# A gated mix of a long convolution and a dilated local attention: the projection's row permutations go to GpSimd's queue, and its last tiles share one buffer

## The chip, the cores and the metric

The kernel runs on one core of a Trainium2 chip. The metric is the device time of one execution in microseconds (us), lower is better. The engines that matter here are TensorE (PE, matrix products), VectorE (DVE) and ScalarE (ACT), which both copy results out of PSUM and do the elementwise work, and two engines that issue transfers here: SyncE (SP) and GpSimd (POOL). Each engine works through its own list of instructions in order, so an instruction that waits holds up everything behind it in its list.

## The reference

The output mixes two branches of the same input, position by position.

```python
x = A_q                                   # [1, 2048, 640]
g = sigmoid((x * gate_w).sum(-1, keepdims=True))
a = q * (irfft(rfft(kv) * rfft(ssm_k)) + kv * ssm_D)   # kv = shifted_conv(k) * v, length 2048 padded to 4096
b = attention(x @ wqkv; 32 heads, window of 8 keys, dilation 2) @ wo
out = g * a + (1 - g) * b
```

Each row of the output thus needs the long convolution's result `y`, times `q` and the gate `g`, plus `(1 - g)` times the row of the projection `b`.

## The kernel before, in words

**The long convolution** is a Fourier transform written as matrix products. The channels go in five groups (`NG = 5`, here g0 to g4). For the data there are per group four units of a first step (`s1_unit`, line 729, source `kv`), four of a second (`s2_unit`, line 747, result in `X[:, 7]`), an elementwise complex product on VectorE (`mults`, lines 866 and 869, four pairs per group), and four units of an inverse step (`inverse1`, line 883). When all of that is done, `inverse2` (line 960) runs over the 16 row positions t, three at a time; its results are copied by ScalarE (line 969), multiplied into `qg` by VectorE (line 972), the projection is added (`adds`, line 1027), and the rows are stored (`store`, line 985). One `X[:, 7]` serves all groups: the second step's copies of g4 may only be written once the products of g3 have been read.

**q** is loaded a second time late (`load_q`, line 923, 16 transfers on SP) into the tile `qg`, which takes the place of `kv`: the load waits for the last unit of the first step, the last reader of `kv`. `qscale` (line 937) multiplies `qg` by the gate on VectorE, 16 instructions.

**The projection** (`outproj`, line 999) makes 16 tiles t, ten matrix products each. ScalarE or VectorE copies a tile, times `1 - g`, into a staging buffer (lines 1010 and 1012). The rows of a tile do not stand on the partitions on which `qg` has them, so each pair of tiles is permuted by four transfers from the staging buffer into the tile `bl` (line 1019), which `adds` then reads. The staging buffer has three places of a pair each: `X[:, 1]` for the first three pairs, then `room`.

**What sets the order.** Nothing is fixed by hand: a planner in plain Python (`Plan`) holds the parts as streams of requests. Every request names an engine ("P", "A", "D", "G" for GpSimd and "S" for SP), a cost in ns, and what it waits for; the planner keeps its own clock per engine and emits next the request with the lowest `start + 120 * priority` (a lower number goes first). Transfers occupy a modelled pipe, and at most eight may be under way for each issuing engine. So a change of an engine, a cost or a priority changes the order of instructions on all engines. PSUM has four places of two banks, which all products share.

Of the kernel before, what the change touches and what calls it, by code (L numbers as in the profile page):

```python
# [10 lines left out]
BF = mybir.dt.bfloat16  # L11
# [6 lines left out]
S = 2048  # L18
# [225 lines left out]
def kernel(  # L244
# [14 lines left out]
    nc = tc.nc  # L259
# [6 lines left out]
    def raw(ap, off, dims):  # L266
        return bass.AP(tensor=ap.tensor, offset=ap.offset + off, ap=dims)
# [11 lines left out]
    def psum(g, name, shape=(128, 2, 512), dt=F32, k=0):  # L279
        t_ = psp.tile(list(shape), dt, name=name, tag=f"ps{g.banks[k]}")  # L280
        return t_
# [11 lines left out]
    G = Gs[:, 0:8192].rearrange("p (a r b) -> p a r b", a=32, r=2)  # L293
# [42 lines left out]
    def ev(name):  # L336
        if name not in E:
            E[name] = Ev()
        return E[name]

    def mark(name, g):
        x = ev(name)
        x.t, x.eng = g.done.t, g.done.eng

    def us(nbytes, run):
        return 1.1 * nbytes / 16.0 / run * (10.0 + run / 24.0)
# [79 lines left out]
    st = {}  # L426
# [145 lines left out]
    def gcol(t):  # L572
        return 8 * (t % 2) + t // 2
# [405 lines left out]
    def store(t):  # L979
        if t in (1, 5):  # L980
            return
        t0 = t - 3 if t < 8 else t - 1
        for gg in range(4):
            eng = nc.gpsimd if t < 8 and gg % 2 else nc.scalar if t == 15 and gg % 2 else nc.sync
            eng.dma_start(raw(outf, (16 * gg + t0) * D, [[64 * D, 32], [1, (t - t0 + 1) * D]]),  # L985
                          st["qg"][32 * gg:32 * gg + 32, t0:t + 1, :].rearrange("p t c -> p (t c)"))

    def outproj():
        yield Req("G", 1.0, [ev("oT"), ev("wo"), ev("gate")])
        oT, wo, bl = st["oT"], st["wo"], st["bl"]  # L990
        stage = None
        for t in range(16):
            u = t // 2
            g = yield Req("P", 1400.0, [ev("i12")] if u >= 6 else [ev("i11")] if u >= 3 else [], take=1, ins=10, pri=8 if t < 6 else None)
            op = psum(g, "op")
            for ft in range(NDT):
                a = oT[:, ft, 0:1]
                for k in range(2):
                    nc.tensor.matmul(op[:, k, 0:320], lhsT=raw(a, HS * (t % 2) + t // 2, [a.ap[0], [8, 128]]),  # L999
                                     rhs=wo[:, ft, 320 * k:320 * k + 320], start=(ft == 0), stop=(ft == NDT - 1))  # L1000
            if u in (3, 6) and t % 2 == 0:
                room = st["p2"].tile([128, 4096], BF, name="room", tag=f"Hs{u // 3}")
                stage = room[:, 0:3840]
            elif t == 0:
                stage = st["X"][:, 1, 0:3840]
            part = stage[:, 1280 * (u % 3):1280 * (u % 3) + 1280].rearrange("p (t c) -> p t c", t=2)
            r = yield Req("AD", dict(A=725.0, D=880.0), [g.done], give=g.banks)
            blt = part[:, t % 2, :].rearrange("p (k c) -> p k c", k=2)
            if r.eng == "A":
                nc.scalar.activation(blt, op[:, :, 0:320], ACT.Copy, scale=omg[:, gcol(t):gcol(t) + 1])  # L1010
            else:
                nc.vector.tensor_scalar(blt, op[:, :, 0:320], omg[:, gcol(t):gcol(t) + 1], None, ALU.mult)
            if t % 2:
                done = r.done
                for gg in range(4):
                    r = yield Req("S", 450.0, [done], move=us(81920, 2560) * 1.5)
                    row = part[gg:gg + 1, 0, 0:1]
                    pitch = row.ap[0][0]
                    nc.sync.dma_start(bl[32 * gg:32 * gg + 32, t - 1:t + 1, :].rearrange("p t c -> p (t c)"),
                                      raw(row, 0, [[4 * pitch, 32], [1, 1280]]))  # L1020
                mark(f"bl{t}", r)

    def adds():
        for t in range(1, 16, 2):
            yield Req("D", 740.0, [ev(f"bl{t}"), ev(f"pr{t}")])
            qg, bl = st["qg"], st["bl"]
            nc.vector.tensor_tensor(qg[:, t - 1:t + 1, :], qg[:, t - 1:t + 1, :], bl[:, t - 1:t + 1, :], ALU.add)  # L1027
            store(t)
# [29 lines left out]
    plan.add(inverse1(), 4)  # L1058
    plan.add(otrans(), 3)
    plan.add(outproj(), 6)  # L1060
    plan.add(load_t(), 0)
    plan.add(load_q(), 1)
# [34 lines left out]
```

## Time and profile before

| what | us |
|---|---|
| median of 3 executions (lowest, highest) | 265.04 (264.39, 267.68) |
| the profiled execution, its own time | 265.23 |
| its span on the core | 263.4 |

The span is what the profile shows from the first to the last instruction; the rest of the profiled execution's time lies around it. The profile's busy times over the span are 214.6 us of PE, 176.2 of DVE, 184.3 of ACT and 51.1 of POOL. These are averages over stages with different limits: the rows of single stretches tell more than the sums.

### The profile page before, as it was taken

The page shows a single profiled execution, that of the slowest core. Times are in us where ns is not written, and L with a number is a line of the kernel's source. Part 1 is how long each engine was busy: PE and PEld are TensorE (multiplying, and loading weights), DVE is VectorE, ACT ScalarE, POOL GpSimd, SP SyncE. Part 2 cuts the span into 40 slices and gives each one's busy share as a digit, 9 for nine tenths or more (in the row PEclk, how much of TensorE's full clock was granted, in tenths as well). Part 3 has the DMA queues.
Part 4 walks back from the last instruction along what each step waited for, and adds up shares of the span by engine and source line. Part 5 has one row for each costly group of instructions (what it writes and reads, how often), then busy time and mean ns, then how long its engine had stood idle before and what let it go on. Part 6 is the DMA issues. An engine that isn't in the chain of part 4 may idle for free.

```text
span 263.4 us, 9665 instructions
## 1 busy us (share of the span) xinstructions
PE 214.6 (81%) x4294; PEld 162.5 (62%) x4294; DVE 176.2 (67%) x223; ACT 184.3 (70%) x220; POOL 51.1 (19%) x107
## 2 busy tenths in 40 slices
PE   7999989999989998888894989999998304996710
PEld 3765544545546675667683888889997204995410
DVE  1658599999998445786785787959851219705851
ACT  4447587577877999999984757889987006886740
POOL 7703704761700643500000000000000000000300
PEclk9999999999999999555579799999999955999575
DMA  6995799877940848989758577415103990111564
GB/s 195 346 357 193 197 281 348 222 183 159 194 130 7 229 92 203 225 146 304 265 124 192 116 146 171 114 55 163 52 2 77 206 170 0 54 50 55 134 194 126
DMA packets 52265, 42.67 MB, mean 162 GB/s; under 512 B 27280, under 2 KB 46864, under 8 KB 52224
## 3 DMA queue, kind: packets, MB, share of 16 engines
q1 hardware_dynamic: 48368, 35.16, 51.5%
q0 software_dynamic: 3760, 6.74, 10.0%
q8 instruction: 33, 0.54, 0.9%
q10 hardware_dynamic: 96, 0.16, 0.2%
q14 instruction: 8, 0.07, 0.1%
HBM read 23.51 MB, written 5.25 MB: 109 GB/s over the span
## 4 chain that ended last, share of the span: by engine, by line
PE 34%; DMA 20%; DVE 18%; issue 14%; ACT 8%; SPq 3%; POOL 2%; DVEq 0%; ACTq 0%; POOLq 0%
PE i L883 8%; DMA qb<-Gs 6%; PE op L999 6%; DMA qg<-in_A_q_dram 5%; PE s L747 5%; ACT ET L670 4%; PE pj L596 3%; PE s L729 3%; DVE pb L474 3%; DVE pa L489 3%; PE psv L534 2%; PE O L696 2%; DVE Hb L273 2%; DVE X L869 2%; DMA Wv<-in_B_wqkv_dram 2%
## 5 line engine op out<-in xcount | busy, mean ns | idle before, releaser
L670 ACT ACTIVATE ET<-sc 128x726 bf16<-128x726 f32 (+1 forms) x80 | 64.5, 865 | 5.5 <-PE sc L662 5.1
L596 PE MATMUL pj<-xT,Wqk 128*128 128x363 bf16 (+3 forms) x250 | 48.4, 343 | 1.8 <-DVE oS L710 1.2
L747 PE MATMUL s<-Am,Gs 64*128 64x64 bf16 x1280 | 30.5, 203 | 21.0 <-ACT X L271 14.1
L747 PEld LDWEIGHTS <-Gs 64*128 64x128 bf16 x1280 | 27.5, 104 | 24.4 <-issue 23.1
L596 PEld LDWEIGHTS <-Wqk 128*128 128x128 bf16 x250 | 23.1, 97 | 20.5 <-DVE oS L710 1.9
L273 DVE CAST Am<-s 128x1024 bf16<-128x1024 f32 x22 | 26.3, 1219 | 7.5 <-PE s L729 7.5
L271 ACT CAST X<-s 128x1024 bf16<-128x1024 f32 x16 | 15.9, 1026 | 16.5 <-DVE X L869 16.5
L985 POOL DMA_DIRECT2D out_dram<-qg x4 | 2.0, 506 | 125.5 <-DVE qg L1027 125.4
L999 PE MATMUL op<-wo,Hb 128*128 128x320 bf16 x160 | 26.4, 314 | 0.0
L534 PE MATMUL psv<-Wv,xT 128*128 128x320 bf16 x170 | 25.2, 299 | 1.0 <-ACT ET L670 0.5
L883 PE MATMUL i<-M,X 128*128 128x128 bf16 x160 | 21.8, 229 | 0.6 <-DVE X L869 0.6
L999 PEld LDWEIGHTS <-Hb 128*128 128x128 bf16 x160 | 21.0, 147 | 1.5
L271 ACT CAST X<-i 128x1024 bf16<-128x1024 f32 x20 | 20.0, 1017 | 2.7 <-PE i L883 2.1
L883 PEld LDWEIGHTS <-X 128*128 128x128 bf16 x160 | 20.6, 150 | 1.3 <-DVE X L869 0.9
L662 PE MATMUL sc<-qb,kb 31*128 31x121 bf16 x544 | 18.6, 245 | 2.7 <-DVE oS L710 1.0
L534 PEld LDWEIGHTS <-xT 128*128 128x128 bf16 x170 | 16.0, 98 | 7.5 <-issue 0.9
L271 ACT CAST Am<-s 128x1024 bf16<-128x1024 f32 x18 | 17.9, 1030 | 2.4 <-PE s L729 2.2
L696 PEld LDWEIGHTS <-ET 128*128 128x128 bf16 x544 | 16.1, 100 | 5.1 <-issue 2.7
L883 PE MATMUL i<-M,Hs 128*128 128x128 bf16 x128 | 18.2, 233 | 0.6 <-ACT Am L271 0.3
L696 PE MATMUL O<-VW,ET 128*128 128x21 bf16 x544 | 16.6, 176 | 2.5 <-ACT ET L670 1.5
L489 DVE TENSOR_TENSOR pa<-pa,pb 128x2560 bf16<-128x2560 bf16 x12 | 17.9, 1489 | 0.3
L662 PEld LDWEIGHTS <-kb 31*128 31x128 bf16 x544 | 10.3, 103 | 12.5 <-issue 8.1
(81 smaller groups left out, 361.0 us busy)
## 6 DMA issues: line engine op xcount, KB each, us to landing
X<-Hs SPq DMA_DIRECT2D x16, 256.0 KB, 4.8
Hb<-in_A_k_dram SPq DMA_DIRECT2D x4, 640.0 KB, 10.4
kv<-in_A_v_dram SPq DMA_DIRECT2D x4, 640.0 KB, 13.5
kv_scr<-Hb SPq DMA_DIRECT2D x8, 320.0 KB, 5.6
Hb<-in_A_ssm_k_dram SPq DMA_DIRECT2D x16, 160.0 KB, 4.2
kv<-kv_scr SPq DMA_DIRECT2D x8, 320.0 KB, 6.6
qg<-in_A_q_dram SPq DMA_DIRECT2D x16, 160.0 KB, 6.0
Gs<-cf_G SPq DMA_DIRECT2D x8, 256.0 KB, 6.8
```

The lines of the kernel that those rows point to most:

```text
L271: nc.scalar.copy(dst, src)
L273: nc.vector.tensor_copy(dst, src)
L474: nc.vector.tensor_tensor(dst[:, t0:t1, :], src, wl[:, j, :].unsqueeze(1).to_broadcast([128, t1 - t0, D]), ALU.mult)
L489: nc.vector.tensor_tensor(pa[:], pa[:], pb[:], ALU.add)
L534: nc.tensor.matmul(ps[:, bb, 0:320], lhsT=xT[:, dt, BP * (b0 + bb):BP * (b0 + bb) + 128], rhs=Wv[:, dt, c0:c0 + 320], start=(dt == 0), sto ...
L596: nc.tensor.matmul(ps[:, i, 0:n], lhsT=Wqk[:, dt, w, 128 * ft:128 * ft + 128], rhs=rhs, start=(dt == 0), stop=(dt == NDT - 1))
L662: nc.tensor.matmul(scs[h4 // 2][:, h4 % 2, BP * bb:BP * bb + BP], lhsT=kb[r:r + DH + NF, 128 * b:128 * b + 128], rhs=qb[r:r + DH + NF, BP ...
L670: nc.scalar.activation(ETs[e][:, :, 0:nw], scs[hf][:, :, 0:nw], ACT.Exp, scale=SCALE)
L696: nc.tensor.matmul(O[:, o0:o0 + 21], lhsT=ET[:, hh, BP * bb:BP * bb + 128], rhs=VW[:, b, 4 * t + h4, :], start=True, stop=True, skip_group ...
L747: nc.tensor.matmul(o, lhsT=G[rows, j, rr, :], rhs=Am[rows, 2 * j + rr, :, :], start=(rr == 0), stop=(rr == 1), tile_position=(64 * c, 0), ...
L883: nc.tensor.matmul(o, lhsT=src[:, c, :, :, 8 * oc + il].rearrange("p q j -> p (q j)"), rhs=M[:, k, :], start=(k == 0), stop=(k == 1), skip ...
L999: nc.tensor.matmul(op[:, k, 0:320], lhsT=raw(a, HS * (t % 2) + t // 2, [a.ap[0], [8, 128]]), rhs=wo[:, ft, 320 * k:320 * k + 320], start=( ...
```

## The change

Three edits. The permuting transfers are issued by GpSimd in place of SP, and are planned on GpSimd's clock and its eight transfers. Four stores (rows up to t = 7) go from GpSimd to SP. The last two pairs of tiles no longer take a third staging buffer but the first two places of `room`, which the pairs of t = 6, 7 and t = 8, 9 used; so their request waits for those pairs' permutations (`bl7`, `bl9`) and not for the inverse step of g2 (`i12`). The request's priority is 8 for t = 6 and 7 (6 before, the stream's own), and 0 for t from 8 on (6 before).

```diff
         for gg in range(4):
-            eng = nc.gpsimd if t < 8 and gg % 2 else nc.scalar if t == 15 and gg % 2 else nc.sync
+            eng = nc.gpsimd if t < 4 and gg % 2 else nc.scalar if t == 15 and gg % 2 else nc.sync
...
-            g = yield Req("P", 1400.0, [ev("i12")] if u >= 6 else [ev("i11")] if u >= 3 else [], take=1, ins=10, pri=8 if t < 6 else None)
+            g = yield Req("P", 1400.0, [ev(f"bl{2 * u - 5}")] if u >= 6 else [ev("i11")] if u >= 3 else [], take=1, ins=10, pri=8 if t < 8 else 0)
...
-            if u in (3, 6) and t % 2 == 0:
-                room = st["p2"].tile([128, 4096], BF, name="room", tag=f"Hs{u // 3}")
+            if t == 6:
+                room = st["p2"].tile([128, 4096], BF, name="room", tag="Hs1")
...
-                    r = yield Req("S", 450.0, [done], move=us(81920, 2560) * 1.5)
+                    r = yield Req("G", 500.0, [done], move=us(81920, 2560) * 1.5)
...
-                    nc.sync.dma_start(bl[32 * gg:32 * gg + 32, t - 1:t + 1, :].rearrange("p t c -> p (t c)"),
+                    nc.gpsimd.dma_start(bl[32 * gg:32 * gg + 32, t - 1:t + 1, :].rearrange("p t c -> p (t c)"),
```

The planner then writes out another order. VectorE's list before, at the place where `kv` has had its last reader (the cast to `Am` is the copy of the last unit of the first step; `Hs` is the product of g3):

```order
L273 CAST X<-s_4233 128x8x128
L273 CAST Am<-s_4303 128x4x64x4
L937 TENSOR_SCALAR qg<-qg,g_nat 128x640 x12
L866 TENSOR_TENSOR Hs<-X,Hs 128x8x128
L869 TENSOR_TENSOR X<-X 128x8x128
```

and of the changed kernel, from the last pair of products of g4 (`sH`) on, which has those of g3 ahead of it:

```order
L866 TENSOR_TENSOR sH<-X,sH 128x8x128
L869 TENSOR_TENSOR X<-X 128x8x128
L937 TENSOR_SCALAR qg<-qg,g_nat 128x640 x16
L972 TENSOR_TENSOR qg<-X,qg 128x3x320 x2
L1027 TENSOR_TENSOR qg<-qg,bl 128x1280
```

All 16 scalings of `qg` now stand behind all the products; before, twelve of them stood ahead of the products of g3, and four ahead of those of g4.

ScalarE's list before, around the copy of the last unit of the first step (`Am<-s_4359`); L1010 is the copy of a projection tile:

```order
L271 CAST X<-s_4314 128x8x128
L1010 ACTIVATE room<-op,omg 128x640
L271 CAST Am<-s_4359 128x4x64x4
L271 CAST X<-s_4395 128x8x128
L271 CAST X<-s_4437 128x8x128
L1010 ACTIVATE room<-op,omg 128x640
L271 CAST X<-s_4486 128x8x128
```

and of the changed kernel, around the same copy (now `Am<-s_4390`):

```order
L271 CAST X<-i_4274 128x128x8
L1010 ACTIVATE room<-op,omg 128x640
L271 CAST X<-i_4305 128x128x8
L1010 ACTIVATE room<-op,omg 128x640
L271 CAST X<-i_4335 128x128x8
L271 CAST Am<-s_4390 128x4x64x4
L1010 ACTIVATE room<-op,omg 128x640
L271 CAST X<-s_4465 128x8x128
```

Ten of the sixteen projection tiles are now computed ahead of the last unit of the first step, where eight were before.

ScalarE's list before, in the last stage (L969 copies a result of `inverse2`):

```order
L271 CAST X<-i_4788 128x128x8
L1010 ACTIVATE room<-op,omg 128x640
L969 CAST X<-i_4817 128x2x3x160
L969 CAST X<-i_4818 128x2x3x160
...
L1010 ACTIVATE room<-op,omg 128x640
L969 CAST X<-i_5146 128x2x3x160
L969 CAST X<-i_5147 128x2x3x160
L1010 ACTIVATE room<-op,omg 128x640
L969 CAST X<-i_5265 128x2x3x160
```

and of the changed kernel:

```order
L271 CAST X<-i_4802 128x128x8
L1010 ACTIVATE room<-op,omg 128x640
L969 CAST X<-i_4832 128x2x3x160
L969 CAST X<-i_4833 128x2x3x160
L1010 ACTIVATE room<-op,omg 128x640
L969 CAST X<-i_4946 128x2x3x160
L969 CAST X<-i_4947 128x2x3x160
```

The last tile's copy has moved from the fourth and fifth round of `inverse2` to behind the first.

## Rows read from the trace of the kernel before

**Rows 1.** The page, its first line.
```profile
span 263.4 us, 9665 instructions
```
**Rows 2.** Windows: start:end, length, busy of each engine (instructions), granted clock, DMA share, GB/s.
```profile
40.00:60.00 20.00, 19.44 (x195) 10.35 (x195) 19.66 (x18) 14.24 (x19) 12.85 (x24) 1.00 0.86 247
171.00:201.00 30.00, 29.13 (x658) 27.04 (x656) 20.61 (x27) 27.05 (x30) 0.00 (x0) 1.00 0.19 60
...
206.50:220.60 14.10, 0.01 (x2) 0.01 (x2) 6.30 (x17) 1.07 (x2) 0.00 (x0) 0.65 0.76 140
220.60:237.10 16.50, 16.22 (x232) 15.67 (x231) 8.43 (x17) 14.50 (x16) 0.00 (x0) 0.89 0.11 41
237.10:251.20 14.10, 10.49 (x533) 7.53 (x532) 9.77 (x14) 9.80 (x12) 2.02 (x4) 0.77 0.37 109
251.20:263.40 12.20, 0.00 (x0) 0.00 (x0) 3.34 (x6) 2.13 (x4) 0.00 (x0) 0.64 0.54 149
```
**Rows 3.** Waits from 150 us on: waiter <- releaser: total us, times, longest us.
```profile
ACT X L271 <- DVE X L869: 16.5, 1, 16.5
DVE qg L937 <- DMA qg<-in_A_q_dram: 14.6, 4, 9.1
PE s L747 <- ACT X L271: 14.1, 1, 14.1
...
DVE qg L1027 <- DMA bl<-room: 4.1, 1, 4.1
```
**Rows 4.** Timeline of VectorE: start, duration, instruction, [idle before it <- releaser].
```profile
195.83 1.22 DVE L273 CAST X<-s 128x1024 bf16<-128x1024 f32 x1 [2.27 <-PE s L747]
...
217.24 0.98 DVE L937 TENSOR_SCALAR qg<-qg,g_nat 128x640 bf16<-128x640 bf16 x3 [0.44 <-DMA qg<-in_A_q_dram]
...
253.75 0.81 DVE L1027 TENSOR_TENSOR qg<-qg,bl 128x1280 bf16<-128x1280 bf16 x1
258.70 0.83 DVE L1027 TENSOR_TENSOR qg<-qg,bl 128x1280 bf16<-128x1280 bf16 x1 [4.14 <-DMA bl<-room]
```
**Rows 5.** Timeline of TensorE's products, same columns.
```profile
198.84 1.58 PE L999 MATMUL op<-wo,Hb 128*128 128x320 bf16 x10
200.36 0.54 PE L729 MATMUL s<-F1b,kv 64*128 64x128 bf16 x8
200.73 0.63 PE L747 MATMUL s<-Am,Gs 64*128 64x64 bf16 x32
...
237.11 1.03 PE L960 MATMUL i<-X,T 32*32 32x160 bf16 x96
...
240.47 0.67 PE L960 MATMUL i<-X,T 32*32 32x160 bf16 x53 [0.29 <-issue]
...
244.20 0.32 PE L960 MATMUL i<-X,T 32*32 32x160 bf16 x21 [1.10 <-issue]
...
249.59 1.61 PE L960 MATMUL i<-X,T 32*32 32x160 bf16 x128
```
**Rows 6.** The chain that ended last: start, time on the chain, engine and line.
```profile
218.21 0.60 DVE Hs L866
...
229.43 3.02 PE i L883 x48
```
**Rows 7.** Timeline of SP's transfer issues: start, time until the last was issued.
```profile
200.93 9.35 SPq L923 DMA_DIRECT2D qg<-in_A_q_dram  x16
...
257.07 3.27 SPq L985 DMA_DIRECT2D out_dram<-qg  x6
```
**Rows 8.** Timeline of ScalarE.
```profile
199.00 1.01 ACT L271 CAST X<-s 128x1024 bf16<-128x1024 f32 x1
200.46 0.79 ACT L1010 ACTIVATE room<-op,omg 128x640 bf16<-128x640 f32 x1 [0.46 <-PE op L999]
```
**Rows 9.** Line 632, earlier transfers of GpSimd's queue: duration in ns min/median/max, then landing.
```profile
L632 POOL DMA_DIRECT2D kb<-Gs x22: 497/499/522, 26.3 to 97.2; - x22
...
DMA to landing us min/median/max: 2.1/4.6/9.4
```

## The prediction

> **What bounds the kernel now.** I read the page for the span [rows 1], then windows over its last third, then the waits of that third and the lists of the engines named there. The reader is to see in the windows that TensorE is busy 29.13 of 30 us from 171 to 201, and then not at all from 206.5 to 220.6; it is filled again until 237.1, three quarters busy in the inverse transform's last step, and idle for the last 12.2 us [rows 2]. So up to 201 the work of TensorE sets the time, and behind it a hole of 14.1 us does, and a tail.
>
> The waits say whose hole it is. VectorE waits 14.6 us for the load of `qg`, ScalarE 16.5 us in one piece for a product of VectorE, TensorE 14.1 us in one piece for a copy of ScalarE [rows 3]. Read backwards it is one chain. The last unit of the first step ends at 200.90 and with it the last read of `kv`; SP issues the load into its place at 200.93 [rows 5, 7]; the last part has landed when the scaling resumes at 217.24 [rows 4]; twelve scalings stand in VectorE's list ahead of the products of g3, though these don't need them, and start at 218.21 [rows 6]; ScalarE must not write the second step's result for g4 before that; and TensorE runs out of PSUM places. The transfer is long, but only VectorE's list makes it everybody's wait.
>
> In the tail VectorE waits 4.1 us for the permutation of the last pair [rows 3]: the sum of the pair before ends at 254.56, the last one at 259.53 [rows 4].
>
> **The change, part by part.** The first edit was about queues, and costs the queues little; what decides is the order that the planner makes of it. All 16 scalings now stand behind the products of g3 and g4, two more projection tiles stand ahead of the last unit of the first step, and the last tile stands behind the first round of `inverse2`. I follow the changed order from 171 on in four terms, with the durations of before.
>
> *To the last unit of the first step.* TensorE is full there [rows 2], so two more tiles at 1.58 from start to end, some 1.5 each from start to start [rows 5], add 3.0 us: 200.9 becomes 203.9. In the stretch where the changed ScalarE list has six copies in a row behind the tile t = 5, at 1.01 each [rows 8], while VectorE does the eight products of g1, 8 x 0.60 [rows 6], PSUM fills and TensorE waits a little; 0.6 us for that, by the 0.87 us that it was idle in the whole 30 us of before. So p = 204.5. Lower bound 203.5 (the tile of t = 4 falls into a short gap at 172), upper bound 206.5 (ScalarE was already busy for 27.05 of 30 us and gets two more copies of 0.79 [rows 2, 8]).
>
> *From there to `inverse2`.* The load of `qg` starts at p as before, but nobody waits behind it. VectorE copies the last result of g3 (0.6 of TensorE [rows 5], then 1.22 [rows 4]) and is at the products at p + 2.0; four pairs of g3 at 2 x 0.60 end at p + 6.8, four of g4 at p + 11.6. ScalarE copies the four results of g4 as the places in `X[:, 7]` come free: p + 8.1. TensorE has its tiles t = 10, 11, 12 in the meantime, then the four inverse units of g3 at 3.02 / 3 = 1.01 [rows 6], the first done at p + 8.5. From here ScalarE is the slower: eight copies of inverse units at 1.01 and two tiles at 0.79 [rows 8], 9.7 us in a row, p + 18.3. TensorE with the four units of g4, which may start at p + 11.6, and the tiles t = 13, 14 comes to p + 18.7. With semaphore times of 0.1 here and there I take 19.0: `inverse2` starts at 223.5, against 237.11 [rows 5]. That is 13.6 us less. All durations are those at full clock: in the hole and just behind it the granted clock was 0.65 and 0.89 [rows 2], and without the hole TensorE has no long idle stretch there.
>
> Does `qg` come in time? The load took 16.3 us (200.93 to 217.24), with the permutations of one pair behind it. Now two or three pairs, 320 KB each against 2,560 KB, move beside it: up to 3 x 2 us if they share the engines fully. It lands between 221 and 227, I take 222.8; the first eight scalings are done before, the last end a us later. VectorE needs them when the first copy of `inverse2` is there, 223.5 + 1.03 + 0.9 = 225.4. So hidden by 1.6 us, with up to 3 us of delay at the upper bound.
>
> *`inverse2` itself.* It took 14.1 us for 512 products and two tiles [rows 2]. TensorE's rows show restarts behind "issue" at 240.47 and 244.20 [rows 5], 3.73 us apart with 128 products and their weight loads between them, though such a piece needs only 1.3 us: the instructions arrive at that pace. The tile t = 14 leaves this stretch, 1.6 us less; the last tile no longer holds a PSUM place over several rounds, for which I take nothing, since the arrival sets the pace. So 12.5 us, between 11.7 (3.73 x 1044 / 256 = 15.2, less the first 3.4 before the first restart, 240.47 - 237.11) and 14.1. TensorE ends at 236.0.
>
> *The tail.* Before, 251.2 to 263.4, 12.2 us. Copies, products and the sum of the last but one pair took from 251.2 to 254.56, 3.4 us. The permutation of the last pair is now issued around 229 and long landed, so the last sum follows at once (0.83). But the four stores of the last but one pair and two of the last one go through SP, 3.27 us for the six [rows 7], and from the last issue at 260.34 to the end of the span there were 3.1 us. 3.4 + 3.3 + 3.1 = 9.8, a gain of 2.4. The sum of the terms is a span of 245.8; with 1.8 us around it (265.23 against 263.4) the execution takes 247.6. The median of before is 0.2 below the profiled execution, so 247.4.
>
> *The permutations on GpSimd.* 32 issues at 0.50 [rows 9] are 16 us of an engine that has nothing else to do after 122 us. Landing is the unknown: earlier transfers of that queue, of 85 KB like these of 80, took 2.1 to 9.4 us, 4.6 in the median [rows 9]. Only one of them has a waiter close by. The inverse units of g1 write over `X[:, 1]`, so their copies on VectorE and on ScalarE wait for the third pair. By my hand count its tile t = 5 is copied at about 182, its fourth issue is done at 184, and the first such copy is due at 186.5 to 187. It lands at 188.6 by the median (1.6 late, but with TensorE's backlog I count half, within the 0.6 above), at 193.4 by the maximum (6.5 late), at 186.1 by the minimum (no wait). I take the median, measured under a DMA share of 0.86 in one of those stretches where the share at this place was 0.19 [rows 2]: if anything it is high. What waits with it is everything behind it in both lists, the products of g2 among it. The waits for `bl7` and `bl9` have over 10 us of slack, and the stores given to SP find an empty queue: no cost.
>
> Here the Trainium skill has a price of its own. Its page DMA: Bandwidth & Descriptors, section Anatomy of one DMA — SWDGE (gpsimd) path, gives about 2.0 us plus the bytes over 436 GB/s; that would be an estimate of 2.2 us for 80 KB, near the minimum of [rows 9] and far from its median, and with it the third pair lands at 186.2 and costs nothing.
>
> **The rivals.** (1) *The permutation of the third pair is late.* At the 9.4 us of [rows 9] it costs up to 6.5 us in the full stretch: 248 to 254. For it speaks that the queue has shown such times; against it the quiet DMA engines. (2) *Only the hole closes.* If `inverse2` and the tail stay as they were, 14.1 + 12.2 behind 223.5 make 249.8, and 251.6 with the rest. For it: the arrival of instructions and SP's stores are not changed. (3) *The hole moves to the load.* `inverse2`'s products on VectorE still need all of `qg`; if the load took twice its 16.3 us beside GpSimd's transfers, it would land at 237, and the time would be about 260, no change. Against it: they are an eighth of its bytes per pair. (4) *Slower than before: GpSimd cannot write its transfers' orders while VectorE works.* Then the third pair holds both copying engines at the place above. It takes 17.8 us to eat the gain and 5.3 more for 2%; the pair would have to land 25 us after its issue at 184, 2.7 times the longest of [rows 9]. That row speaks against it: 497 to 522 ns for an issue, though in the stretch from 40 to 60 VectorE was busy for 19.66 of 20 us. The Trainium skill's page SBUF — State Buffer, section Who interferes with whom, has this lock, for certain forms of VectorE instructions; [rows 9] shows none of it, but the forms at work then were others than the copies and scalings here. (5) *The edit is only a change of queue:* the order shown says otherwise, so this has no chance of its own.
>
> **How the numbers follow.** My forecast, 244 to 250, has a chance of 0.62. Rival 1 has 0.11, rival 2 0.14, rival 3 0.05, rival 4 0.04, and 0.04 remain for a time under 244, with a shorter first term and the early landing. The range of 8 in 10 takes in the forecast, rival 2 and most of rival 1, with the bounds of the terms: 243 to 254. A measurement of this kernel can tell about 2% from no change, so faster means below 259.7: the forecast, rivals 1 and 2 and the early case, 0.91. Rival 3 is "same", 0.05; rival 4 is slower, 0.04.
>
> **What would show it.** Right: no idle stretch of TensorE over 2 us between 171 us and `inverse2`; the scalings behind the products of g4 in VectorE's timeline; the load of `qg` begun 3 to 4 us later than before; the last sum on VectorE without a wait for `bl`. A wait of VectorE or ScalarE for `bl<-X` would show rival 1, `inverse2` over 14 us rival 2, VectorE's products of `inverse2` waiting for `qg` rival 3, issues of GpSimd well over 0.5 us rival 4. Wrong I'd be above all if ScalarE, with its lists so full, lets TensorE wait in several places of the middle.

## The result and the profile after

The changed kernel takes 250.52 us in the median (250.15 to 250.99) against 265.17 for the kernel before: a ratio of 0.9433, with a 95% interval of 0.9368 to 0.9498. The prediction was 247.4, with 243 to 254 as its range. The profiled execution took 250.15 us with a span of 248.4. Medians and ranges, here and below, are of all executions of a kernel, while ratios, and differences between two kernels, are of those in the faster of the chip's two states.

The windows of the changed kernel, with the same columns as [rows 2], cut at its own stages:

```profile
171.00:201.00 30.00, 28.75 (x583) 26.98 (x574) 20.55 (x27) 25.60 (x28) 6.25 (x12) 1.00 0.21 70
...
203.30:222.00 18.70, 18.35 (x363) 17.27 (x363) 15.15 (x30) 15.97 (x18) 5.49 (x11) 1.00 0.94 195
222.00:235.00 13.00, 7.65 (x522) 5.94 (x516) 9.89 (x18) 9.29 (x11) 3.11 (x6) 0.84 0.26 81
235.00:239.50 4.50, 0.00 (x0) 0.00 (x0) 4.43 (x8) 1.86 (x4) 0.00 (x0) 0.50 0.83 224
239.50:245.40 5.90, 0.00 (x0) 0.00 (x0) 0.00 (x0) 0.00 (x0) 0.00 (x0) 0.50 0.57 138
245.40:248.40 3.00, 0.00 (x0) 0.00 (x0) 0.00 (x0) 0.00 (x0) 0.00 (x0) 0.50 0.21 52
```

The hole of 14.1 us is gone: from the last unit of the first step to `inverse2` TensorE is busy for 18.35 of 18.70 us, at a granted clock of 1.00, where before the same work straddled a stretch at 0.65 and one at 0.89 [rows 2]. What is new stands in the last two rows: for 8.9 us no compute engine does anything at all.

VectorE's timeline, against [rows 4]:

```profile
203.02 2.36 DVE L273 CAST X<-s 128x1024 bf16<-128x1024 f32 x2 [6.60 <-PE s L747]
205.29 0.68 DVE L866 TENSOR_TENSOR Hs<-X,Hs 128x1024 bf16<-128x1024 bf16 x1
...
214.93 2.45 DVE L937 TENSOR_SCALAR qg<-qg,g_nat 128x640 bf16<-128x640 bf16 x8
220.63 0.39 DVE L937 TENSOR_SCALAR qg<-qg,g_nat 128x640 bf16<-128x640 bf16 x1 [3.26 <-issue]
221.32 2.16 DVE L937 TENSOR_SCALAR qg<-qg,g_nat 128x640 bf16<-128x640 bf16 x7 [0.29 <-DMA qg<-in_A_q_dram]
223.98 0.66 DVE L972 TENSOR_TENSOR qg<-X,qg 128x960 bf16<-128x960 bf16 x1 [0.51 <-ACT X L969]
...
237.88 1.55 DVE L1027 TENSOR_TENSOR qg<-qg,bl 128x1280 bf16<-128x1280 bf16 x2
```

The products of g3 start at 205.29, 12.9 us earlier than [rows 6] has them, and all 16 scalings stand behind those of g4. VectorE still waits for the load of `qg`, 3.26 us and 0.29 (the first row names no releaser, but it stands, as the 4.83 us of the kernel before did, between the eighth and the ninth scaling), with nothing behind it that others need by then: the first product of `inverse2` then waits 0.51 us for ScalarE, not for `qg`. The two last sums end at 239.43, without a wait for `bl`.

TensorE in `inverse2`, against [rows 5]:

```profile
221.90 1.02 PE L960 MATMUL i<-X,T 32*32 32x160 bf16 x96
...
225.15 1.34 PE L960 MATMUL i<-X,T 32*32 32x160 bf16 x128 [0.26 <-issue]
229.15 1.32 PE L960 MATMUL i<-X,T 32*32 32x160 bf16 x125 [2.66 <-issue]
...
233.15 1.58 PE L960 MATMUL i<-X,T 32*32 32x160 bf16 x125 [1.35 <-issue]
```

Restarts behind "issue" (the engine waits for nothing that the profile shows) come at 225.15, 229.15 and 233.15, 4.0 us apart, with some 128 products between them that take 1.3 us. TensorE ends at 234.73.

SP's issues (against [rows 7]), one row of SP's own waits, and GpSimd's drains, instructions that stand at the end of its program (the long one, 10.07 us, is the first, at 230.1):

```profile
203.36 10.22 SPq L923 DMA_DIRECT2D qg<-in_A_q_dram  x16
229.30 16.02 SPq L985 DMA_DIRECT2D out_dram<-qg  x20
```
```profile
SPq L985 <- DMA out_dram<-qg: 2.4, 1, 2.4
```
```profile
L1092 POOLq DRAIN  x3: 46/242/10072, 230.1 to 248.1; - x3
```

The 20 stores keep SP busy until 245.32, 5.9 us beyond the last sum; behind the last issue come 3.1 us, as before. That is the idle end of the windows. The drain becomes important below.

The permuting transfers (line 1019, as [rows 9]):

```profile
L1019 POOL DMA_DIRECT2D bl<-X x12: 525/528/574, 164.3 to 183.0; - x12
...
DMA to landing us min/median/max: 2.1/2.6/8.2
```

They are issued in 0.53 us each, and all 32 of the line land after 2.6 us in the median. The rows of two pairs, the third and the one that is issued beside the load of `qg`:

```profile
L1019 POOL DMA_DIRECT2D bl<-X x4: 525/526/528, 181.4 to 183.0; - x4
...
DMA to landing us min/median/max: 2.3/2.8/3.3
```
```profile
L1019 POOL DMA_DIRECT2D bl<-room x4: 525/526/528, 208.7 to 210.3; - x4
...
DMA to landing us min/median/max: 7.6/8.1/8.2
```

The third pair has thus landed about a microsecond before VectorE makes the first copy over its place, at 186.51, and no copy waits for `bl<-X`.

### The profile page after: what moved, and what is told of

Read it like the earlier page. It is cut to its first block, busy times and chain, and to the rows that moved or that the text cites. A ratio compares the mean times of both kernels' runs of the same rounds, so it can differ in the third digit from the quotient of the medians.

```text
span 248.4 us, 9692 instructions
## 1 busy us (share of the span) xinstructions
PE 211.4 (85%) x4294; PEld 160.9 (65%) x4294; DVE 178.4 (72%) x225; ACT 182.5 (73%) x218; POOL 67.7 (27%) x137
## 3 DMA queue, kind: packets, MB, share of 16 engines
q0 software_dynamic: 4688, 9.03, 14.1%
## 4 chain that ended last, share of the span: by engine, by line
PE 49%; DVE 18%; ACT 10%; issue 8%; DMA 7%; SPq 2%; POOL 1%; DVEq 0%; ACTq 0%
PE pj L596 11%; PE op L999 7%; PE i L883 7%; PE psv L534 6%; ACT ET L670 6%; PE s L747 5%; PE O L696 4%; DVE pb L474 4%; DVE pa L489 3%; PE s L729 3%; PE sc L662 3%; DMA qg<-in_A_q_dram 2%; DMA Wv<-in_B_wqkv_dram 2%; DVE Hb L273 2%; SPq L923 2%
## 5 line engine op out<-in xcount | busy, mean ns | idle before, releaser
L747 PE MATMUL s<-Am,Gs 64*128 64x64 bf16 x1280 | 29.7, 201 | 6.4 <-issue 4.1
L747 PEld LDWEIGHTS <-Gs 64*128 64x128 bf16 x1280 | 26.5, 102 | 10.2 <-issue 9.0
L273 DVE CAST Am<-s 128x1024 bf16<-128x1024 f32 x20 | 23.9, 1219 | 6.3 <-PE s L729 6.3
L999 PE MATMUL op<-wo,Hb 128*128 128x320 bf16 x160 | 25.1, 304 | 0.0
L883 PE MATMUL i<-M,X 128*128 128x128 bf16 x160 | 21.3, 227 | 0.5 <-DVE X L869 0.5
L271 ACT CAST Am<-s 128x1024 bf16<-128x1024 f32 x20 | 20.0, 1030 | 2.4 <-PE s L729 2.2
L271 ACT CAST X<-i 128x1024 bf16<-128x1024 f32 x19 | 19.1, 1012 | 3.4 <-PE i L883 2.3
L1019 POOL DMA_DIRECT2D bl<-X x12 | 6.3, 532 | 56.0 <-ACT X L1010 56.0
L662 PE MATMUL sc<-qb,kb 31*128 31x121 bf16 x544 | 18.6, 245 | 2.3 <-DVE oS L710 1.0
L1019 POOL DMA_DIRECT2D bl<-room x20 | 10.4, 526 | 33.9 <-ACT room L1010 33.9
L883 PE MATMUL i<-M,Hs 128*128 128x128 bf16 x128 | 17.1, 228 | 0.4 <-ACT X L271 0.4
## 6 DMA issues: line engine op xcount, KB each, us to landing
kv<-in_A_v_dram SPq DMA_DIRECT2D x4, 640.0 KB, 12.2
```

The source lines that it names most:

```text
L271: nc.scalar.copy(dst, src)
L273: nc.vector.tensor_copy(dst, src)
L662: nc.tensor.matmul(scs[h4 // 2][:, h4 % 2, BP * bb:BP * bb + BP], lhsT=kb[r:r + DH + NF, 128 * b:128 * b + 128], rhs=qb[r:r + DH + NF, BP ...
L747: nc.tensor.matmul(o, lhsT=G[rows, j, rr, :], rhs=Am[rows, 2 * j + rr, :, :], start=(rr == 0), stop=(rr == 1), tile_position=(64 * c, 0), ...
L883: nc.tensor.matmul(o, lhsT=src[:, c, :, :, 8 * oc + il].rearrange("p q j -> p (q j)"), rhs=M[:, k, :], start=(k == 0), stop=(k == 1), skip ...
L1019: nc.gpsimd.dma_start(bl[32 * gg:32 * gg + 32, t - 1:t + 1, :].rearrange("p t c -> p (t c)"), raw(row, 0, [[4 * pitch, 32], [1, 1280]]))
```

## The experiments

The kernels ran in three groups, each on one chip with the kernel before beside it; they are compared within their group or by their ratio to the kernel before. The changed kernel ran again in the second and the third: 252.02 us (249.15 to 255.41, ratio 0.9403, 0.9342 to 0.9464; I had expected 250 to 251) and 252.47 us (250.08 to 253.92, ratio 0.9485, 0.9413 to 0.9557; expected 250 to 252.5). So two medians of six that differ by under a microsecond say nothing.

### What carries the gain: order, queue, or places

Theory: VectorE's order alone makes and closes the hole. Rival: GpSimd's queue, or the two places and the priorities, are needed. Four kernels of one group.

**The order alone**, in the kernel before:

```diff
-            r = yield Req("D", 230.0, [ev(f"qg{t // 8}"), ev("gate")])
+            r = yield Req("D", 230.0, [ev(f"qg{t // 8}"), ev("gate"), ev("mult4")])
```

> The kernel before with one edit: the scalings of qg are requested only when the products of g4 are planned, so that all 16 stand behind them in VectorE's list. Queues, staging buffers and priorities stay as before. Theory (the hole is made by VectorE's order alone): the idle stretch of TensorE goes, inverse2 begins near 222 in place of 237, the tail stays as before with the wait for the last pair on SP; 249 to 253 us. Rival (GpSimd's queue or the staging places open the way): TensorE still idles over 10 us, 262 us or more.

It took 249.28 us, a ratio of 0.9309 (0.9239 to 0.9379). `inverse2` begins at 221.38. Its scalings, its last sum and the permutations of its last pair, from the timelines of VectorE and of SP:

```profile
213.79 2.46 DVE L937 TENSOR_SCALAR qg<-qg,g_nat 128x640 bf16<-128x640 bf16 x8
...
243.69 0.82 DVE L1027 TENSOR_TENSOR qg<-qg,bl 128x1280 bf16<-128x1280 bf16 x1 [4.48 <-DMA out_dram<-qg]
```
```profile
240.20 1.75 SPq L1019 DMA_DIRECT2D bl<-room  x3
242.06 3.26 SPq L985 DMA_DIRECT2D out_dram<-qg  x6
```

One waiting condition in the kernel before gives all of the change's gain, with the permutations on SP. The planner moves little else for it: by the trace the lists of SP and GpSimd are those of before, two copies pass from ScalarE to VectorE, and some projection tiles shift among the inverse units. The wait of the last sum is still there, 4.48 us. The row names a store as releaser, but the sum reads `bl`, and its last permutations were issued on SP until 241.95, behind a row of stores.

**The order back**, in the changed kernel:

```diff
-                r = yield Req("D", 660.0, [ev(f"u{g}out{jb}"), ev(f"h{g}out{jb}")])
+                r = yield Req("D", 660.0, [ev(f"u{g}out{jb}"), ev(f"h{g}out{jb}")] + ([ev("qs11")] if g == 3 else [ev("qs15")] if g == 4 else []))
```

> The changed kernel with the order of before forced on VectorE: the products of g3 wait for the twelfth scaling and those of g4 for the sixteenth. The permutations stay on GpSimd, the places and priorities as changed. Theory (order): the hole is back, inverse2 begins some 15 us later than in the changed kernel; 262 to 268 us. Rival (queue): it stays near 250.

It took 267.24 us, a ratio of 0.9986 (0.9936 to 1.0037): the whole gain is lost, with queue, places and priorities as changed. By the trace the lists of SP and GpSimd are those of the changed kernel; ScalarE has three of its tile copies earlier in its list. Its waits show the chain of [rows 3] again:

```profile
DVE qg L937 <- DMA qg<-in_A_q_dram: 13.9, 4, 7.3
ACT X L271 <- DVE X L869: 13.4, 1, 13.4
PE s L747 <- ACT X L271: 12.3, 2, 11.9
```

**The queue alone**, in the kernel before:

```diff
-                    r = yield Req("S", 450.0, [done], move=us(81920, 2560) * 1.5)
+                    r = yield Req("G", 500.0, [done], move=us(81920, 2560) * 1.5)
...
-                    nc.sync.dma_start(bl[32 * gg:32 * gg + 32, t - 1:t + 1, :].rearrange("p t c -> p (t c)"),
+                    nc.gpsimd.dma_start(bl[32 * gg:32 * gg + 32, t - 1:t + 1, :].rearrange("p t c -> p (t c)"),
```

> The kernel before with the permutations planned and issued on GpSimd, and nothing else changed. The planner then puts one scaling ahead of the products of g4 and 15 behind, and the last tile's copy at the very end of ScalarE's list. Theory (order): no hole over 4 us, but a wait of VectorE at the end for the last pair's permutation; 250 to 256 us. Rival (the gain needs the places and the priority): 260 us or more.

252.47 us, a ratio of 0.9413 (0.9325 to 0.9501). It gains, because the planner, with the permutations on another clock, put one scaling ahead of the products of g4 and 15 behind.

**The places and priorities alone** (the other edits of `outproj` in the diff and the store edit; permutations planned and issued on SP):

> The kernel before with the two places of one buffer and the priorities of the change, but the permutations planned and issued on SP. The planner puts eleven scalings ahead of the products of g3 and one ahead of those of g4. Theory (order): the hole stays, 261 to 267 us. Rival (the places or the priority carry the gain): 255 us or less.

265.45 us, a ratio of 0.9975 (0.993 to 1.002): no change. Eleven scalings stand ahead of the products of g3, and ScalarE waits 15.7 us, TensorE 13.9, as in [rows 3]:

```profile
ACT X L271 <- DVE X L869: 15.7, 1, 15.7
PE s L747 <- ACT X L271: 13.9, 1, 13.9
```

**The same order with the permutations on SP** (second group): the changed kernel, planned as it is, and only the issuing engine put back.

```diff
-                    nc.gpsimd.dma_start(bl[32 * gg:32 * gg + 32, t - 1:t + 1, :].rearrange("p t c -> p (t c)"),
+                    nc.sync.dma_start(bl[32 * gg:32 * gg + 32, t - 1:t + 1, :].rearrange("p t c -> p (t c)"),
```

> The changed kernel, planned as it is, so with the same order on TensorE, VectorE and ScalarE, but with the permuting transfers issued on SP. Theory (the queue by itself is worth nothing): 249.5 to 252 us. Rival (GpSimd's queue matters, since on SP the permutations stand behind the load of qg and ahead of the stores): 253 us or more.

250.61 us, a ratio of 0.9407 (0.9351 to 0.9464), beside 0.9403 of the changed kernel on the same chip. VectorE's and ScalarE's lists are the same in both traces. The issuing queue itself is worth nothing that these runs can tell.

### What the tail is made of

The end was 3 us later than predicted, and SP's list of stores was the suspect. The trace of the changed kernel tells which semaphore each transfer raises: those of SP and ScalarE take eight semaphores in turn, and SP's second store of t = 11 takes the one that ScalarE's first store of t = 15 took before it. The wait of 2.4 us above fits it: ScalarE's store is issued at 239.46 and lands 1.8 us later, and there SP's last nine stores start, 2.6 us behind the end of the sums for t = 13.

```profile
239.46 0.85 ACTq L985 DMA_DIRECT2D out_dram<-qg  x2
```
```profile
L985 ACTq DMA_DIRECT2D out_dram<-qg x2: 374/378/383, 239.5 to 239.9; - x2
...
DMA to landing us min/median/max: 1.8/1.8/1.8
```
```profile
241.26 4.05 SPq L985 DMA_DIRECT2D out_dram<-qg  x9
```

**No store on ScalarE, by way of GpSimd** (second group):

```diff
-            eng = nc.gpsimd if t < 4 and gg % 2 else nc.scalar if t == 15 and gg % 2 else nc.sync
+            eng = nc.gpsimd if (t < 4 or t == 15) and gg % 2 else nc.sync
```

> The changed kernel with the two stores of ScalarE's queue issued on GpSimd. SP keeps its 20 stores. Theory (SP's second store of t = 11 waits until a last store of ScalarE has landed, because SP and ScalarE count in the same eight semaphores): this wait of 2.4 us goes and SP ends its issues 2.4 us sooner; 247.5 to 248.7 us. Rival (the tail is set by the number of stores on SP or by their landing): 250 to 251, as the changed kernel.

255.75 us, a ratio of 0.9563 (0.9506 to 0.962): 4.1 us slower than the changed kernel beside it, against both expectations. SP has no wait for a store left, and its list takes 14.51 us in place of 16.02 (1.5 us less, where 2.4 were expected), yet the span ends at 253.3:

```profile
230.96 14.51 SPq L985 DMA_DIRECT2D out_dram<-qg  x20
```
```profile
L1092 POOLq DRAIN  x3: 46/108/10232, 242.3 to 253.0; - x3
```

**Every second store on GpSimd** (second group):

```diff
-            eng = nc.gpsimd if t < 4 and gg % 2 else nc.scalar if t == 15 and gg % 2 else nc.sync
+            eng = nc.gpsimd if gg % 2 else nc.sync
```

> The changed kernel with every second store on GpSimd, 12 stores on each of the two queues and none on ScalarE. Theory (behind the last sum the tail is SP's list of stores at 0.46 us each, and the wait): SP's last issue comes a microsecond behind the last sum, and the end 3 us behind that; 245 to 246.5 us. Rival (the tail is set by landing on full DMA engines): 247.5 us or more.

254.36 us, a ratio of 0.9521 (0.9462 to 0.9579), slower by 2.8 us than the changed kernel beside it. Both queues have issued their last store by 240.0, and the span ends at 251.1. SP, GpSimd and GpSimd's drain:

```profile
228.81 10.74 SPq L985 DMA_DIRECT2D out_dram<-qg  x12
```
```profile
238.02 1.97 POOL L985 DMA_DIRECT2D out_dram<-qg  x4 [1.03 <-DVE qg L1027]
```
```profile
L1092 POOLq DRAIN  x3: 46/108/10941, 239.4 to 250.9; - x3
```

The two fell for a reason that neither expectation had: behind its last transfer GpSimd drains for 10 to 11 us, and the program does not end before that. From 239.4 the drain of 10.94 us reaches 250.3, and the span ends 0.8 us later; from 242.3 one of 10.23 reaches 252.5, and the span ends at 253.3. In the changed kernel GpSimd's last transfer is a store of t = 3, the drain of 10.07 us begins at 230.1, and is over when SP is not. The kernel with the queue alone has it too, its last pair being permuted at 238.5 to 240.6: a drain of 10.20 us from 240.1, a span of 251.1.

**No store on ScalarE, all of them on SP** (third group):

```diff
-            eng = nc.gpsimd if t < 4 and gg % 2 else nc.scalar if t == 15 and gg % 2 else nc.sync
+            eng = nc.gpsimd if t < 4 and gg % 2 else nc.sync
```

> The changed kernel with the two stores of ScalarE's queue on SP, so 22 stores on SP and GpSimd's list ending with the stores of t = 3 as before. Theory (two things were mixed in the two earlier store experiments: the wait of SP for ScalarE's store goes, but GpSimd ends its list with a drain of about 10 us behind its last transfer, which became the end): without transfers late on GpSimd, the 2.4 us wait goes and two more issues of 0.46 come; 1 to 2 us below the changed kernel. Rival (the drain had nothing to do with it; stores away from ScalarE cost 3 us or more by themselves): 3 us or more above the changed kernel.

251.68 us, a ratio of 0.9455 (0.9383 to 0.9527), 0.5 us below the changed kernel on this chip, for the 1 to 2 expected. The sign is that of the theory, the size is within the scatter, and by the time alone it stays open. The mechanism shows in SP's list: 22 stores in 14.65 us where 20 took 16.02, with no wait for a store among its waits. The list ends 4.8 us behind the last sum, where it ends 5.89 us behind it in the changed kernel's trace above and 5.87 in that of the second group. The rival is out: no extra 3 us.

```profile
230.30 14.65 SPq L985 DMA_DIRECT2D out_dram<-qg  x22
```

**Fewer stores** (third group), the same and

```diff
-        if t in (1, 5):
+        if t in (1, 5, 9):
             return
-        t0 = t - 3 if t < 8 else t - 1
+        t0 = t - 3 if t < 12 else t - 1
```

> As the kernel beside it, and the rows of t = 8 to 11 are stored by four transfers of double size behind the sum of t = 11 in place of eight. Theory (SP's list of issues is the tail): four issues fewer and no idle wait, SP's last issue about 3 us sooner than in the changed kernel; 2.5 to 3.5 us below it. Rival (landing sets the tail): no better than the kernel beside it.

248.89 us (247.85 to 251.05), a ratio of 0.9392 (0.9327 to 0.9458), beside 252.47 and 0.9485 of the changed kernel. It is 3.1 us faster, though the intervals of the ratios overlap; its slowest execution, 251.05, lies below the changed kernel's median. SP's list is over at 243.92 though the last sum of this execution is a microsecond later, at 240.37: 3.6 us between them, against 4.8 in the kernel beside it and 5.9 in the changed one.

```profile
230.78 13.14 SPq L985 DMA_DIRECT2D out_dram<-qg  x18
```

It has the lowest time of the versions of the changed kernel that were run. By the ratio to the kernel before, the one waiting condition alone was at least as good: 0.9309 (0.9239 to 0.9379) against 0.9392.

## Why the prediction was right, and where a term was off

| term | predicted | measured |
|---|---|---|
| end of the last unit of the first step | 204.5 | 203.3 |
| `inverse2` begins | 223.5 | 221.9 |
| TensorE ends | 236.0 | 234.7 |
| last sum ends | about 240.2 | 239.4 |
| span ends | 245.8 | 248.4 |

**The chain was right, and shown from both sides.** VectorE's order makes the hole: imposed on the kernel before, the late scalings give the gain (249.28); taken from the changed kernel, they take it away (267.24). The load of `qg` is no shorter than before, 18.0 us from the first issue to the resumed scaling. It only has nothing behind it.

**To the last unit of the first step** it was 2.4 us more in place of 3.6, so the load also began 2.4 us later and not the 3 to 4 given as a sign. The 1.2 us say nothing against the term: in the traces of six other runs with the same lists on ScalarE and VectorE up to there, this unit ends between 202.5 and 205.0. **From there to `inverse2`** the hand count gave 19.0, the trace 18.6, and all those six 18.6 too. **`qg` in time:** I had 1.6 us of cover; VectorE had scaled the last row 0.51 us before the first product could start. The load took 1.7 us more than before (18.0 against 16.3 [rows 4, 7]) for the 2.0 counted. That the transfers beside it slow it is not shown by itself. The cover is no safe one: in the changed kernel's trace of the second group the load took 19.8 us, and the first product came directly behind the last scaling, without a gap.

**`inverse2`** took 12.8 us for 12.5, and 12.0 in the second group's trace. The restarts were 4.0 us apart here and 3.5 there, around the 3.73 of [rows 5]. With two tiles in it the stage took 14.1 us before and 14.4 with the order alone; so the tile taken out was worth 1.3 to 2.4 us for the 1.6 of the sum. (Its lower bound should read 11.8, by its own figures.)

**The permutations on GpSimd** cost nothing, as forecast. The landing of 2.6 us was between the minimum and the median of [rows 9], and the third pair's 2.3 to 3.3 us were no wait for anyone. By the formula of the Trainium skill's page DMA: Bandwidth & Descriptors, section Anatomy of one DMA — SWDGE (gpsimd) path, it would be an estimated 2.2 us for 80 KB. The trace agrees with that page where the DMA engines are quiet (2.1 to 2.3 us for the pair issued from 171.08 on), and not beside the load of `qg`, at a DMA share of 0.94, where a pair took 7.6 to 8.2 us. Rival 1 fell with the landing of the third pair. Rival 4 needed issues well over 0.5 us, and they took at most 0.574; but only the last issue of the pair at 218.77 ran beside a scaling, so for that form the rival was hardly put to the test.

**The step that failed is the tail.** The prediction said that "the stores given to SP find an empty queue: no cost", and counted six stores, 3.3 us, behind the sum of the last but one pair. By that SP's list ends 2.5 us behind the last sum (236.0 + 3.4 + 3.3 = 242.7, against 240.2); it ended 5.9 us behind it. (SP got two stores more, those of t = 7 from GpSimd, 20 in place of 18; the text ahead of the prediction says four.) The sums now come so close together that SP is behind from t = 7 on: the 14 stores of t = 9 to 15 were issued from 236.6 on, at 0.46 us each, with the 2.4 us wait for ScalarE's store in the middle. From TensorE's end to the end of the span it was 13.7 us and not 9.8. Of these 3.9 us, 3.4 are SP's list behind the last sum, and 0.5 lie ahead of that sum.

The runs show two parts of the 3.4: with ScalarE's stores on SP the wait is gone and the list ends 1.1 us sooner behind the last sum, with four stores fewer another 1.2. The last 1.1 us no run takes apart.

The 3.9, less the 1.3 that the earlier terms were too long, are the 2.6 by which the span was missed. That the 1.3 came off is luck, since the end of the first step moves by more than that from execution to execution. The 250.52 lies in the stated range, but above the 244 to 250 that the forecast itself had, and nearer to rival 2's 251.6. Rival 2 had the right place (the tail) for the wrong reason: it expected the old tail of 12.2 us to stay, not a new one of 13.7.

## What to carry to other kernels

When a planner orders the instructions, a change of a queue or a priority is judged by the order that comes out: find the one engine whose list has an instruction waiting for a long transfer ahead of work that doesn't need it, and move that; here a single waiting condition did all of it. When such a hole closes, the work behind it comes more densely, so queues that were idle enough before (here SP's stores) have to be counted again at the new pace. Before a late transfer is given to another queue, look at what that queue does at the end of the program (here a drain that was longer the more transfers the queue had), and at which semaphores it shares.

## What was not expected of the hardware

GpSimd's long drain at the end of its program goes by the number of transfers that GpSimd issued in the whole program. Counted in the 13 traces:

| transfers on GpSimd | drain, us | kernels |
|---|---|---|
| 84 | 7.46, 7.47 | places and priorities alone; permutations on SP |
| 86 | 7.65, 7.65 | before; order alone |
| 116 | 10.07 in all six | changed (three traces); order back; stores on SP; fewer stores |
| 118 | 10.20, 10.23 | queue alone; no store on ScalarE |
| 126 | 10.94 | every second store on GpSimd |

That is about 0.08 us for each further transfer. The changed kernel pays 2.4 us more for it than the kernel before, hidden because its drain begins at 230.1. In three kernels (queue alone, no store on ScalarE, every second store on GpSimd) the drain was the end of the program, and their spans end 0.8 us behind it. Why it grows so no run here tells; the queue's packets (3,664 to 5,040) grow along with the transfers, and the runs don't separate the two.
